# Moving weight loads, mask rows and transposes by a few chunks in a fused hash-attention and gated-MLP kernel

## The chip, the cores and the metric

The kernel runs on one core of a Trainium2 chip. The time is device microseconds (us) of one execution. It was taken five times; the median counts. One further execution was recorded by the hardware profiler, and all durations below are from that one.

## The reference, cut to what matters

Attention comes first: 4 batches of 8 heads, 768 positions, 64 numbers per head. Every query and key gets a 6-bit hash (the signs of its products with `proj`), and a query sees only the keys with its own hash. The result, regrouped as 3072 tokens of 512 numbers, goes through a gated MLP with a gated residual.

```python
q_bits = (np.einsum('bhsd,dk->bhsk', q, proj) > 0)      # the same for k
mask = q_bucket[:, :, :, None] == k_bucket[:, :, None, :]
scores = np.where(mask, scale * q @ k^T, -1e9)
attn = softmax(scores) @ v                               # then to x: 3072 x 512
...
ffn_out = (gelu(x @ w_gate) * (x @ w_val)) @ w_out
out = x + sigmoid(x @ w_res) * ffn_out
```

## The kernel before, in words

**Pairs and chunks.** Heads are taken two at a time: 16 pairs, four to a batch, numbered from 0 in the code, so the "third pair" is pair 2 and the "fifth pair" is pair 4. A pair's scores are cut into nine chunks. The main loop (L575 to L595) runs over 144 slots, one chunk each: slot 9p is the first chunk of pair p. A slot issues the score matmuls of its chunk (`scores`, L368: four or eight matmuls for the two heads into a PSUM tile `sp`, then one exponential on ScalarE into `e`), then the tasks listed for that slot, then MLP matmuls of the batch before as filling, then the product of an earlier chunk's `e` with the values (`values`, L341).

**The mask is folded into the score matmul.** Each head has 64 rows of transposed q or k and 7 more "mask rows" made of the hash bits. The first head of pair p lies in the tiles `aug[p, side]` (rows 0 to 63, mask rows from row 64), the second in `second[p % 4][side]` (rows 64 to 127, mask rows in rows 0 to 6). So a pair's first score matmuls need both `aug` tiles complete, and the next ones both `second` tiles.

**How a pair is prepared.** q and k come in by `load` (L79; DMAs of 384 KB issued from SyncE's queue, SP). GpSimd (POOL) casts them to bf16 (`cast`, L169). For pairs 4 and up a DMA transpose issued from SP puts them into `aug` (`transpose_dma`, L186), and POOL copies the second head's rows into `second` (`move_second`, L190). VectorE transposes the unrounded q and k in 32x32 blocks (`blocks`, L210), TensorE computes the hashes of two pairs at once (`hash_half`, L240), and `spread` (L265) lays the bits out in the tile `bits` with three copies on VectorE. `mask_rows` (L286 to L290) then issues four small DMAs from SP, 10.5 KB each: two into the `aug` tiles, then two into the `second` tiles. POOL's `values_prep` (L464) makes the value operand: one cast and a sum in three steps; pairs 2 and 3 sum on VectorE instead.

**What sets the order.** Nothing reorders the program: each engine and each DMA queue executes in the order written. `at(slot, f, ...)` (L448) appends a task to a slot by hand; tasks of one slot run in the order in which the `at` lines stand. An engine that waits for nothing runs ahead of the others, so the slot of a POOL or SP task gives its place in that queue and no time.

**Buffers.** `ldv` has two buffers, so the value load of pair 3 waits for POOL's sum of pair 1's values, `ld` has three, `aug` four, `second` four. SP's DMAs take eight completion semaphores in turn; an issue waits for the DMA eight places before it.

**Weights.** `load_w` (L160) issues the next of twelve MLP weight DMAs from POOL's own DMA queue: gate and value weights in four column quarters each (384 KB), the residual weights, the output weights in thirds. Four are issued early, eight in slot 39. `gate_val` (L383) first uses them in slot 39, which is the fourth slot of the second batch; the rest of the kernel alternates such gate/value stages with batches of attention that are filled up with `project` (L407).

Of the kernel before, what the change touches and what calls it, by code (L numbers as in the profile page):

```python
# [17 lines left out]
def kernel(  # L18
# [96 lines left out]
    for sides in ((0, 0, 1, 1), (0, 1, 0, 1)):  # L115
# [5 lines left out]
        for side, val in ((0, 1.0), (1, -NBITS / 4.0)):  # L121
            i, j = [j for j in range(4) if sides[j] == side]
# [325 lines left out]
    def at(slot, f, *args):  # L448
        if f in (hash_half, spread, transpose_pe):
            uses_tp.add(slot)  # L450
        tasks[slot].append(lambda: f(*args))
        busy[slot] += cost.get(f, 0.0)
# [55 lines left out]
    at(1, spread, 1, 0, 4, ROW)  # L508
    at(2, spread, 1, 4, T, TP)
    at(2, mask_rows, 1)  # L510
    at(6, values_prep, 1)

    for i in range(4):
        x = (2 + i // 2, i % 2)
# [6 lines left out]
        at(8 + dh, hash_half, 2, dh, ROW)  # L521
    for i, s in enumerate((10, 11, 12)):
        at(s, spread, 2, 4 * i, 4 * i + 4, (TP, ROW, TP)[i])
    for p in (2, 3):
        at(12, mask_rows, p)
    for p in (2, 3):
        at(6 * p - 2, values_cast, p)
        at(3 * p + 8, values_sum, p, nc.vector)
# [6 lines left out]
    for p in range(4, NPAIR, 2):  # L535
        s0 = NCH * (p - 2)
        for i in range(4):
            x = (p + i // 2, i % 2)
            at(s0 + i, cast, x)
            at(s0 + 2 + i, blocks, x)  # L540
            at(s0 + 4 + 2 * (i // 2), transpose_dma, x)
            at(s0 + 8 + i, move_second, x)
        for dh in range(2):
            at(s0 + 7 + dh, hash_half, p, dh)
        for i, s in enumerate((9, 12, 13)):
            at(s0 + s, spread, p, 4 * i, 4 * i + 4)
        at(s0 + 13, mask_rows, p)
        at(s0 + 15, mask_rows, p + 1)
        at(s0 + 12, values_prep, p)
        at(s0 + 17, values_prep, p + 1)  # L550
        at(s0 + 10, load, p + 1, (2,))
        if p + 2 < NPAIR:
            at(s0 + 5, load, p + 2, (0, 1))
            at(s0 + 8, load, p + 3, (0, 1))
            at(s0 + 15, load, p + 2, (2,))
    for s in [13, 14, 15, 16] + 8 * [39]:
        at(s, load_w)

    LEAD = 4
# [3 lines left out]
    for b in range(1, B):  # L563

        s0 = b * per_batch
# [9 lines left out]
    for s in range(NSLOT):  # L575
        p, c = divmod(s, NCH)
# [56 lines left out]
```

## Time and profile before

| what | value |
|---|---|
| median of 5 runs | 364.36 us (363.98 to 364.92) |
| the profiled execution, its time | 364.36 us |
| its span, first to last instruction | 362.6 us |
| TensorE (PE) busy | 345.4 us, 95% |
| ScalarE (ACT) busy | 211.8 us, 58% |
| VectorE (DVE) busy | 147.2 us, 41% |
| POOL busy | 123.2 us, 34% |
| mean granted TensorE clock | 0.992 |
| DMA traffic | 38.02 MB, mean 105 GB/s |

The page gives for each engine its busy time and share; below that, the span in 40 slices of 9.07 us, with a digit for the busy tenths. "PEclk" there is the clock that TensorE was granted; one slice of the first ten stands at 8 tenths, the others there at 9. In the table of groups the last column is the time in which the engine stood idle before an instruction, and what ended that. TensorE's share is 95%, so the engine itself is the limit almost everywhere, and what can be won or lost lies in the few stretches where it waits. Of the span, 1.8 us (364.36 less 362.6) lie around the first and last instruction.

### The profile page before, as it was taken

The page shows a single profiled execution, that of the slowest core. Times are in us where ns is not written, and L with a number is a line of the kernel's source. Part 1 is how long each engine was busy: PE and PEld are TensorE (multiplying, and loading weights), DVE is VectorE, ACT ScalarE, POOL GpSimd, SP SyncE. Part 2 cuts the span into 40 slices and gives each one's busy share as a digit, 9 for nine tenths or more (in the row PEclk, how much of TensorE's full clock was granted, in tenths as well). Part 3 has the DMA queues.
Part 4 walks back from the last instruction along what each step waited for, and adds up shares of the span by engine and source line. Part 5 has one row for each costly group of instructions (what it writes and reads, how often), then busy time and mean ns, then how long its engine had stood idle before and what let it go on. Part 6 is the DMA issues. An engine that isn't in the chain of part 4 may idle for free.

```text
span 362.6 us, 7415 instructions
## 1 busy us (share of the span) xinstructions
PE 345.4 (95%) x3026; PEld 203.7 (56%) x3078; DVE 147.2 (41%) x200; ACT 211.8 (58%) x234; POOL 123.2 (34%) x178
## 2 busy tenths in 40 slices
PE   8896999999999999999999999999999999999994
PEld 4554566666465566666455556665556555565442
DVE  7864544343343344333443434333442123333343
ACT  4886887324778788232877777332778875232210
POOL 7996297000448258200046457400025112000000
PEclk9999899999999999999999999999999999999998
DMA  7579929998206932920004954510002210000012
GB/s 241 197 258 184 263 102 148 185 208 176 57 23 149 266 99 79 228 107 0 2 3 126 203 168 127 119 42 2 1 2 81 63 51 31 29 2 0 31 59 85
DMA packets 50201, 38.02 MB, mean 105 GB/s; under 512 B 28244, under 2 KB 47096, under 8 KB 50168
## 3 DMA queue, kind: packets, MB, share of 16 engines
q1 hardware_dynamic: 43752, 32.31, 33.3%
q0 software_dynamic: 6336, 5.24, 9.9%
q8 instruction: 24, 0.39, 0.5%
q14 instruction: 9, 0.07, 0.1%
q10 hardware_dynamic: 80, 0.00, 0.0%
HBM read 29.36 MB, written 6.29 MB: 98 GB/s over the span
## 4 chain that ended last, share of the span: by engine, by line
PE 86%; ACT 4%; DMA 3%; DVE 2%; POOL 2%; issue 2%; SPq 0%; DVEq 0%; ACTq 0%; POOLq 0%
PE sp L393 34%; PE fps L425 17%; PE sp L374 14%; PE av L355 9%; PE rps L415 5%; PE hs L248 3%; ACT e L378 3%; DMA ld<-in_q_dram 2%; PE av L348 2%; PE spr L261 2%; DMA second<-bits 1%; POOL second L192 1%; ACT th L418 1%; PE tp L200 1%; DVE o L430 1%
## 5 line engine op out<-in xcount | busy, mean ns | idle before, releaser
L378 ACT ACTIVATE e<-sp 128x1024 bf16<-128x1024 f32 x144 | 144.8, 1024 | 39.0 <-PE sp L374 30.8
L399 ACT ACTIVATE gt<-sp 128x768 bf16<-128x768 f32 x48 | 38.9, 811 | 82.9 <-PE sp L393 82.9
L402 DVE SCALAR_TENSOR_TENSOR hh<-gt,sp 128x768 bf16<-128x768 bf16 x48 | 45.8, 954 | 81.7 <-PE sp L393 81.7
L425 PE MATMUL fps<-wo,hh 128*128 128x512 bf16 x276 | 72.8, 378 | 0.8
L393 PE MATMUL sp<-x_sb,wg 128*128 128x512 bf16 (+1 forms) x377 | 70.0, 325 | 0.5
L432 POOL TENSOR_TENSOR o<-o,x_tok 128x512 f32<-128x512 f32 x18 | 20.8, 1155 | 145.7 <-DVE o L430 81.8
L393 PE MATMUL sp<-x_sb,wv 128*128 128x512 bf16 (+1 forms) x375 | 69.8, 324 | 0.5
L355 PEld LDWEIGHTS <-e 128*128 128x128 bf16 x1152 | 52.3, 98 | 30.7 <-issue 9.4
L355 PE MATMUL av<-va,e 128*128 128x65 bf16 x1152 | 58.7, 194 | 1.0 <-ACT e L378 0.5
L374 PE MATMUL sp<-aug,aug 71*128 71x512 bf16 x192 | 55.3, 328 | 3.8 <-DMA aug<-bits 2.0
L393 PEld LDWEIGHTS <-wg 128*128 128x128 bf16 x384 | 37.4, 98 | 25.0 <-issue 0.3
L393 PEld LDWEIGHTS <-wv 128*128 128x128 bf16 x384 | 37.4, 98 | 24.5
L374 PE MATMUL sp<-second,second 128*128 128x256 bf16 (+1 forms) x172 | 47.4, 321 | 0.6 <-DMA second<-bits 0.6
L425 PEld LDWEIGHTS <-hh 128*128 128x128 bf16 x288 | 27.6, 97 | 27.6
L430 DVE SCALAR_TENSOR_TENSOR o<-th,fps 128x512 f32<-128x512 f32 x24 | 16.4, 685 | 56.2 <-PE fps L425 56.2
L192 POOL COPY second<-aug 64x768 bf16<-64x768 bf16 x32 | 25.7, 825 | 33.9 <-DMA aug<-nat 25.1
L212 DVE STREAM_TRANSPOSE t<-ld 128x768 f32<-128x768 f32 x32 | 29.5, 952 | 0.0
L415 PE MATMUL rps<-wr,x_sb 128*128 128x512 bf16 x93 | 24.4, 379 | 0.2
L418 ACT ACTIVATE th<-rps 128x512 f32<-128x512 f32 x24 | 14.3, 595 | 16.3 <-PE rps L415 13.0
L374 PEld LDWEIGHTS <-second 128*128 128x128 bf16 x192 | 18.9, 98 | 6.0 <-issue 2.4
L268 DVE CAST bits<-spr 128x512 bf16<-128x512 f32 (+1 forms) x23 | 15.4, 679 | 12.5 <-PE spr L261 12.5
L374 PEld LDWEIGHTS <-aug 71*128 71x128 bf16 x192 | 16.3, 97 | 6.6 <-DMA aug<-bits 2.1
(56 smaller groups left out, 216.6 us busy)
## 6 DMA issues: line engine op xcount, KB each, us to landing
ld<-in_q_dram SPq DMA_DIRECT2D x16, 384.0 KB
ld<-in_k_dram SPq DMA_DIRECT2D x16, 384.0 KB
ldv<-in_v_dram SPq DMA_DIRECT2D x16, 384.0 KB
out_dram<-o SPq DMA_DIRECT2D x24, 256.0 KB
wg<-in_moe_w_gate_dram POOLq DMA_DIRECT2D x4, 384.0 KB, 6.6
wv<-in_moe_w_val_dram POOLq DMA_DIRECT2D x4, 384.0 KB, 9.3
wo<-in_moe_w_out_dram POOLq DMA_DIRECT2D x3, 512.0 KB, 23.7
wr<-in_moe_w_res_dram POOLq DMA_DIRECT2D x1, 512.0 KB, 17.6
```

What stands on the lines that cost most here:

```text
L192: eng.tensor_copy(second[x[0] % NM][x[1]][D:P], aug[x][D:P])
L212: nc.vector.transpose(tt.rearrange("p c h n -> p (c h n)"), raw[x].rearrange("p c d -> p (c d)"))
L355: nc.tensor.matmul(o[:, qt, :], e[:, off:off + P], va[:, hi, jt, 0:D + 1], start=False, stop=(jt == T - 1), skip_group_check=True)
L374: nc.tensor.matmul(sp[:, off:off + nq * P], ks[0:n, jt, :], qs[0:n, qt0:qt0 + nq, :], start=True, stop=True)
L378: nc.scalar.activation(e, sp, AF.Exp, scale=float(ALPHA))
L393: nc.tensor.matmul(sp[:, c0:c1], w[:, kk, bass.ts(m, P)], xs[:, kk, c0:c1], start=(kk == 0), stop=(kk == KM - 1))
L399: nc.scalar.activation(gt, sp[:, 0:S], AF.Gelu)
L402: nc.vector.scalar_tensor_tensor(hh[:, m, :], gt, 0.5, ps[1][:, 0:S], op0=ALU.mult, op1=ALU.mult)
L415: nc.tensor.matmul(rps, x_sb[b][:, kk, t, :], wr[:, kk, :], start=(kk == 0), stop=(kk == KM - 1))
L425: nc.tensor.matmul(fps, hh[:, m, bass.ts(t, P)], wo[:, m, :], start=(m == 0), stop=(m == KF - 1))
L430: nc.vector.scalar_tensor_tensor(o, th, 1.0, fps, op0=ALU.add, op1=ALU.mult)
L432: last.tensor_add(o3, o3, x_tok[b][:, :, t, :])
```

## The change

Five places of the schedule move; no instruction is added or taken away.

```diff
-    at(6, values_prep, 1)
+    at(8, values_prep, 1)
...
-    for p in (2, 3):
-        at(12, mask_rows, p)
+    at(12, mask_rows, 2)
+    at(14, mask_rows, 3)
...
     for p in range(4, NPAIR, 2):
         s0 = NCH * (p - 2)
         for i in range(4):
             x = (p + i // 2, i % 2)
...
-            at(s0 + 4 + 2 * (i // 2), transpose_dma, x)
-            at(s0 + 8 + i, move_second, x)
+            at(s0 + (8 if p == 4 else 4) + i // 2, transpose_dma, x)
+            at(s0 + (11 if p == 4 else 8) + i, move_second, x)
...
-    for s in [13, 14, 15, 16] + 8 * [39]:
+    for s in [17, 18, 19, 20] + 8 * [39]:
         at(s, load_w)
```

What this makes of the queues, as the built program has them:

- POOL, from the second head's copy of pair 2 on. Before: copy, value cast and sum of pair 1 (four instructions), three copies, value cast of pair 2, weight loads 1 to 3, value cast of pair 3, weight load 4, four casts of pairs 4 and 5. After: three copies, value cast and sum of pair 1, one copy, value casts of pairs 2 and 3, weight load 1, cast, load 2, cast, load 3, cast, load 4, cast.
- SP: the mask rows of pairs 2 and 3 follow each other as before (no SP task lies in slots 13 and 14). Then, before: value load of pair 4, two transposes of pair 4, two loads of pair 6, two transposes of pair 5, two loads of pair 7. After: value load of pair 4, loads of pair 6, transposes of pair 4, loads of pair 7, transposes of pair 5.
- POOL's copies of pair 5 come after the value cast and sum of pair 4 instead of ahead of them.
- For pairs 6, 8, 10, 12 and 14 the transposes of the odd pair behind it (7, 9, ...) stand one slot earlier, and so ahead of the two loads of slot s0+5.

## Prediction

> **What bounds the kernel now.** I read TensorE's own waits first, then the stretches they fall in, then the time-ordered list of instructions there, then the DMA queues of that stretch. TensorE is 95% busy, so its waits are nearly all there is to win. The list of its waits over the whole run:
>
> ```profile
> PE sp L374 <- DMA aug<-bits: 2.0, 1, 2.0
> PE sp L374 <- ACT e L378: 1.5, 6, 0.4
> ...
> PE sp L374 <- DMA second<-bits: 0.6, 1, 0.6
> ```
>
> The columns are total us, times, longest. One event of 2.0 and one of 0.6 us, both for mask rows. The stretches around it (busy us of PE, PEld, DVE, ACT, POOL, then granted clock, DMA share, GB/s):
>
> ```profile
> 27.50:31.50 4.00, 3.68 (x58) 2.90 (x57) 3.27 (x3) 3.79 (x5) 3.98 (x7) 1.00 1.17 159
> 31.50:35.90 4.40, 1.75 (x23) 0.97 (x21) 0.15 (x2) 1.91 (x3) 1.53 (x2) 1.00 1.31 208
> 35.90:39.30 3.40, 3.01 (x23) 1.94 (x24) 3.37 (x5) 2.97 (x4) 0.00 (x0) 0.50 1.55 199
> ```
>
> TensorE works 1.75 of 4.40 us, and in the next 3.4 us its clock is halved. Who issued what, in order of time:
>
> ```profile
> 25.88 0.97 POOL L162 DMA_DIRECT2D wg<-in_moe_w_gate_dram  x1
> ...
> 26.68 1.53 SPq L290 DMA_DIRECT2D aug<-bits  x2
> 26.85 0.75 POOL L162 DMA_DIRECT2D wv<-in_moe_w_val_dram  x1
> ...
> 28.30 1.70 SPq L290 DMA_DIRECT2D second<-bits  x2
> ...
> 33.58 0.39 PE L374 MATMUL sp<-aug,aug 71*128 71x512 bf16 x1 [2.02 <-DMA aug<-bits]
> ...
> 34.52 0.38 PE L374 MATMUL sp<-second,second 128*128 128x512 bf16 x1 [0.55 <-DMA second<-bits]
> ```
>
> Pair 2's four mask rows are issued from 26.68 to 30.0, just after the weight loads. In the trace's completion counts they land at 31.34, 33.54, 33.75 and 34.39: 4.7 to 6.0 us after issue (26.68, 27.52, 28.30, 29.32). Pair 4's rows, issued from 49.60 in an empty stretch, land 1.9 to 2.0 us after issue. So the weights cost each row 2.7 to 4.1 us. The queues from 28 to 36 us (packets, MB, share of 16 engines):
>
> ```profile
> q0 software_dynamic: 1941, 1.45, 121.0%
> q1 hardware_dynamic: 94, 0.08, 3.7%
> ```
>
> q0 carries POOL's weights, q1 all of SP's DMAs: the rows are a trickle behind a saturated queue.
>
> **What is there to win.** TensorE was ready at 31.56 (end of the value matmuls that start at 31.16). ScalarE, the bound of this stage at 0.9 to 1.0 us per chunk, waits 2.49 us and resumes at 35.00. After that, at half clock, it waits 0.24 and 0.92 us more; some 0.3 to 0.5 of it would be there anyway (x's transposes fall there), so the clock costs about 0.8. Full prize: 2.5 + 0.8 = 3.3 us.
>
> **The change, step by step.**
>
> *When the first weight load now goes out.* POOL does not wait for slots; it runs ahead. Pair 2's first copy starts at 18.87. Now two more copies come first (0.77 each by their spacing), so pair 1's cast and sum start at 21.3 instead of 19.76, and its first sum ends at about 23.1 instead of 21.55. SP's value load of pair 3 waits for that sum: 23.1 instead of 21.58. Pair 2's load of the same kind, issued at 18.33 into idle engines, landed at 21.77, after 3.44 us; so pair 3's lands at about 26.6. POOL, free at 25.9, now waits 0.7 us for it, because the value cast of pair 3 stands ahead of the weights. The cast takes 0.77, and the first load is issued at W = 27.4 instead of 25.88. The next follow every 1.7 us (0.75 to 0.97 issue + 0.8 cast): 29.1, 30.7, 32.2. The move is four slots in the program but 1.5 us in time for the first load.
>
> *When the rows land.* SP issues pair 2's rows at the same times, since they wait for VectorE's bits (26.66). The loads of pairs 4 and 5 in q1 now end near 28.7 instead of 28.2; the first row slips behind them, to about 29. Second row, 27.52: W+0.1. The nearest row of the trace is pair 5's last mask row, issued 0.2 us after a weight load (55.12 and 54.92): it landed at 59.14, 4.0 us later, while its forerunner, issued 0.5 us ahead of the load, took 1.9. So the second row lands between 29.4 and 31.5, in time either way. The `second` rows, 28.30 and 29.1, are W+0.9 and W+1.7. With one load ahead, as pair 2's first row had it (4.7 us), they land at 33.0 and, one more turn of the queue (0.8 us by the spacing of the rows' packets), 33.4 to 33.8. Bounds for the last: 31.0 if nothing delays it, 35.1 if it gets the 6.0 us of the row that met two loads. I take 33.4: the second load is issued in the same 0.1 us, so half the contention of before.
>
> The Trainium skill speaks of a smaller delay. DMA: Bandwidth & Descriptors, section on queues, rings and completion order: each engine takes turns between queues packet by packet, about 9 to 17 descriptors each. At 79 ns per weight descriptor (the trace) a row would wait at most 1.3 us: the last row would land at 29.1 + 1.9 + 1.3 = 32.3 and the change would win 2.2 us of the stall. The rows of before waited 2.7 to 4.1; I go by them.
>
> *What TensorE does with it.* The `aug` matmul starts at 31.56, no wait. The `second` matmul starts at 33.4 instead of 34.52: 1.1 us. The idle time shrinks from 2.57 (2.02 + 0.55) to some 1.5 us, in one gap.
>
> *Does the clock still drop?* TensorE: Matmul & The Clock Gate, section on HAM oscillation, says that idle gaps must stay under about 3.4 us. By that the clock would not have dropped before either, with gaps of 2.0 and 0.55, and there would be nothing to regain here. The trace shows 0.50 for 3.4 us after them; PE was busy about half of the window before. With 1.5 us idle it is busy over that. I take it that the clock holds, at 6 in 10: +0.8 us.
>
> Sum: 1.1 + 0.8 = 1.9 us off the span, 362.6 to 360.7; with the 1.8 us around it, 362.5 us. The profiled execution's own time equals the median.
>
> *What costs nothing, and its cover.* Pair 1's value sum ends at 24.1 instead of 22.6; its first reader, TensorE, comes at 26.2: without that 2.1 us of cover each us would be a us of TensorE. Pair 3's mask rows keep their place on SP; they are read in slot 27 (about 45.9) and landed at 37.1. The weight loads of slot 39 stand after the same POOL work; wv's third quarter landed at 65.5 and is needed near 74, 6 us of cover even when TensorE comes 2 us earlier. For pairs 6 and up the odd pair's transposes move ahead of two loads; those are issued 1.2 to 13 us later (the first two at about 75 instead of 61.7) and are cast at 112. Later ones have 20 us or more (118.5 and 139.7). In those stages TensorE waits for no DMA at all.
>
> *What has less cover.* Pair 4's transposes now stand behind two loads on SP. Before, they landed near 41 and POOL's copies of pair 4 ended at 42.6. Pair 4's mask rows, which overwrite rows those copies read, are issued at 49.60, when the bits are ready; their last lands at 53.88, and TensorE reads them at 54.52: 0.6 us of cover. With TensorE 1.9 us earlier the rows fall due at 47.7. Behind the weights (ending 1.5 us later) and two loads of 1.1 us, the transposes land at about 44.5; copies end at 46.1. Cover: 1.6 us, and the 0.6 behind it.
>
> **Rivals.**
>
> *Half of it.* The last row also meets the second load, lands at 34 to 34.4, and the clock drops as before: gain 0 to 1.1 us, 363.7. For: both are issued within 0.1 us. Against: before, three loads were out by 28.3, now one. 0.25.
>
> *All of it.* Pair 3's value load lands later than I think (one of its engines came 0.8 us late before), W passes 28.5, the rows get through: 361.2. Against: the row at W'+0.2 lost 2 us even so. 0.12.
>
> *Slower: the fifth pair's rows come late.* DMA transposes issued behind loads under weight traffic were held up: 6.9 and 6.0 us at 63.0 and 70.0, against 1.3 in quiet. Behind pair 4's two transposes SP still has two loads, two transposes and a value load to issue, 4.0 us together, before pair 4's mask rows; the last of those is issued 2.4 us after the first and lands 1.9 after that. They are needed at 54.5 less 1.9 = 52.6. So the second transpose's issue may end at 52.6 - 8.3 = 44.3 without harm; past that each us is a us, and with 0.8 for the clock the gain is gone at 45.4. With both held up it ends at 34.6 + 12.9 = 47.5: 3.2 lost, plus 0.8, less 1.9: 366.5. Against: the weights end near 39.5 here, where in that stretch they lasted to 86. 0.16.
>
> *It does not do what it says*, because POOL's run-ahead undoes the move wholly (W near 26): 364.4. 0.05.
>
> **How the numbers follow.** Forecast 0.42 (361.9 to 363.1), half 0.25, all 0.12, late rows 0.16, nothing 0.05. This kernel can be told from no change at about 0.2%, 0.7 us: faster below 363.6, slower above 365.1. Faster: 0.40 + 0.11 + 0.12 = 0.63; slower 0.17; same 0.20. The range takes in "all" at its likely value and the milder half of the late rows: 361.0 to 365.2.
>
> **What would show it.** Right: the first weight issue near 27.4 behind a cast of pair 3, the `aug` matmul of slot 18 without a wait, the `second` one waiting 1 to 1.8 us, clock 1.00 up to 40 us, copies of pair 4 over by 46.5. Wrong: W before 26.5 or after 28.5; rows that land 2 us after issue although a weight load is ahead; a wait of TensorE near 52 us; or any DMA wait after 90 us.

## The result and the profile after

The changed kernel takes 363.2 us (median of 43 runs, 361.23 to 366.32). The kernel before, measured beside it, takes 364.09 us (80 runs, 363.02 to 365.7). The ratio is 0.9977, with a 95% interval from 0.9967 to 0.9986: 0.9 us faster, where 1.9 was forecast (362.5 us). The profiled execution took 363.49 us with a span of 361.7.

First TensorE's waits for the whole run:

```profile
PE sp L374 <- DMA second<-bits: 1.7, 1, 1.7
...
PE sp L374 <- ACT e L378: 1.3, 5, 0.4
```

The wait of 2.0 us for `aug<-bits` is gone. The one for `second<-bits` has grown from 0.6 to 1.7 us. Together 2.6 us became 1.7. No other wait for a DMA's mask rows has come up, at slot 36 or anywhere behind it. The same stretches as before:

```profile
27.50:31.50 4.00, 3.68 (x56) 2.83 (x56) 3.07 (x3) 3.59 (x4) 3.96 (x6) 1.00 0.93 175
31.50:35.90 4.40, 2.66 (x32) 1.59 (x29) 0.69 (x3) 2.74 (x4) 2.73 (x4) 0.87 1.20 181
35.90:39.30 3.40, 3.18 (x35) 1.99 (x35) 3.40 (x4) 2.49 (x4) 0.00 (x0) 0.67 1.22 259
```

TensorE is busy for 2.66 of the 4.40 us instead of 1.75. Yet the granted clock, the third number from the end, still falls: 0.87 and then 0.67. Who issued what, in order of time:

```profile
26.87 1.49 SPq L290 DMA_DIRECT2D aug<-bits  x2
26.95 0.83 POOL L293 CAST va<-ldv 128x768 bf16<-128x768 f32 x1 [0.81 <-DMA ldv<-in_v_dram]
...
27.72 0.97 POOL L162 DMA_DIRECT2D wg<-in_moe_w_gate_dram  x1
...
28.46 1.44 SPq L290 DMA_DIRECT2D second<-bits  x2
...
31.83 0.38 PE L374 MATMUL sp<-aug,aug 71*128 71x512 bf16 x1
...
33.87 0.39 PE L374 MATMUL sp<-second,second 128*128 128x512 bf16 x1 [1.67 <-DMA second<-bits]
...
35.43 0.58 PE L374 MATMUL sp<-aug,aug 71*128 71x256 bf16 x2
...
49.28 1.02 ACT L378 ACTIVATE e<-sp 128x1024 bf16<-128x1024 f32 x1 [0.39 <-PE sp L374]
...
57.78 1.02 ACT L378 ACTIVATE e<-sp 128x1024 bf16<-128x1024 f32 x1 [0.54 <-PE sp L374]
```

The first weight load goes out at 27.72, behind the cast that waits 0.81 us for pair 3's values. In the completion counts the `aug` rows land at 29.74 and 29.94, in time; the `second` rows at 33.65 and 33.83, which is 5.2 and 4.6 us after their issue. The two matmuls at 35.43 take 0.58 us together instead of 0.38, as the same pair does at 30.91: that is the reduced clock.

**A ruler for all the runs.** The last two of these lines are the exponentials of slots 31 and 39. In the kernel before they stand at

```profile
50.16 1.02 ACT L378 ACTIVATE e<-sp 128x1024 bf16<-128x1024 f32 x1 [0.39 <-PE sp L374]
...
58.66 1.02 ACT L378 ACTIVATE e<-sp 128x1024 bf16<-128x1024 f32 x1 [0.54 <-PE sp L374]
```

Profiles differ by up to 1.2 us in when pair 2's mask rows are ready (first issue from 25.81 to 26.99). So I count from that issue: 23.48 and 31.98 us before, 22.41 and 30.91 after. By slot 31 the change has gained 1.07 us, and by slot 39 it still has 1.07. The span shows 0.9, since the rows were issued 0.19 later in this profile. The slot of a reader shows what was won at slot 18; the later one shows what was given back at slot 36, where pair 4's mask rows are first read.

| kernel | gained by slot 31, us | by slot 39, us | median us (runs) | ratio to before [95%] |
|---|---|---|---|---|
| the change | 1.07 | 1.07 | 363.2 (43) | 0.9977 [0.9967, 0.9986] |
| e1_loads_only | 2.35 | -1.55 | 363.87 (14) | 0.9991 [0.9969, 1.0013] |
| e2_no_transposes | 0.96 | 0.95 | 363.49 (14) | 0.9991 [0.9974, 1.0008] |
| e3_fifth_pair_only | -0.38 | -0.38 | 363.88 (14) | 0.9995 [0.9983, 1.0007] |
| e4_loads_behind_copies | 3.70 | 0.84 | 365.14 (22) | 1.0035 [1.0015, 1.0054] |
| e5_loads_plus_late_kv | 1.24 | 1.24 | 362.97 (22) | 0.9961 [0.9947, 0.9976] |
| e6_gate_late_kv | 3.70 | 0.80 | 364.22 (22) | 1.0004 [0.9991, 1.0017] |
| e7_after_filler | 2.47 | 1.79 | 362.58 (22) | 0.9964 [0.9947, 0.998] |
| e8_after_late_kv | 1.11 | 1.11 | 362.85 (22) | 0.9972 [0.9953, 0.9991] |
| e9_loads_kv_filler | 2.11 | 2.10 | 361.5 (5) | 0.9933 [0.9921, 0.9945] |
| e10_before_filler | 0.83 | 0.82 | 363.01 (13) | 0.9969 [0.9959, 0.9978] |
| e11_after_kv_filler | 2.07 | 2.06 | 362.77 (12) | 0.9961 [0.9943, 0.9979] |
| e12_late_loads_late_kv | 3.70 | 2.36 | 361.9 (7) | 0.9943 [0.9916, 0.997] |

The gains are of one profiled execution each, the medians and ratios of many. Each kernel was timed beside runs of the kernel before, whose medians lay between 364.09 and 364.36. Two of the 22 runs of e4 (368.5 and 368.93) lay over 1.5% above its fastest and stand in its median, but not in its ratio.

### The profile page after: what moved, and what is told of

The parts are those of the page before. It is cut to its first block, busy times and chain, and to the rows that moved or that the text cites. A ratio compares the mean times of both kernels' runs of the same rounds, so it can differ in the third digit from the quotient of the medians.

```text
span 361.7 us, 7415 instructions
## 1 busy us (share of the span) xinstructions
PE 345.3 (95%) x3026; PEld 203.4 (56%) x3078; DVE 147.2 (41%) x200; ACT 211.8 (59%) x234; POOL 123.5 (34%) x178
## 4 chain that ended last, share of the span: by engine, by line
PE 87%; ACT 4%; DMA 3%; DVE 2%; POOL 2%; issue 2%; SPq 0%; DVEq 0%; ACTq 0%; POOLq 0%
PE sp L393 34%; PE fps L425 17%; PE sp L374 14%; PE av L355 9%; PE rps L415 5%; PE hs L248 3%; ACT e L378 3%; DMA ld<-in_q_dram 2%; PE av L348 2%; PE spr L261 2%; DMA second<-bits 1%; POOL second L192 1%; ACT th L418 1%; PE tp L200 1%; DVE o L430 1%
## 5 line engine op out<-in xcount | busy, mean ns | idle before, releaser
L355 PEld LDWEIGHTS <-e 128*128 128x128 bf16 x1152 | 52.3, 98 | 30.7 <-issue 9.4
```

Of the source, the lines that this page charges most:

```text
L355: nc.tensor.matmul(o[:, qt, :], e[:, off:off + P], va[:, hi, jt, 0:D + 1], start=False, stop=(jt == T - 1), skip_group_check=True)
```

## The experiments

My theory after the result: the stall at slot 18 is the mask rows' wait behind the weights. What the change should have won beyond 1.07 us went to the halved clock, which the remaining idle time still triggers. Rivals: part of the gain is given back at slot 36 by the fifth pair's late rows; or the part that moves the transposes takes it away.

### Which part does it?

**e1_loads_only**, the weight loads alone:

```diff
-    for s in [13, 14, 15, 16] + 8 * [39]:
+    for s in [17, 18, 19, 20] + 8 * [39]:
```

> Only the first four weight loads move (slots 17 to 20); value sum of pair 1, mask rows and transposes stay as before. Theory A (the rows of pair 2 land earlier because fewer weight loads are queued ahead of them): pair 3's value load keeps its issue at 21.6 us and lands near 26.1, so the first weight load goes out near 26.9 instead of 27.7 with the whole change; it meets all four rows of pair 2, and TensorE's `second` matmul of slot 18 starts between 33.9 and 34.5. Gain 0 to 0.6 us, less than the whole change. Theory B (the gain comes from the order of transposes and loads on SP): no gain, 0.0 us, `second` matmul at 34.5. If the loads' slots alone carry the change: the same 0.9 us.

Slot 18 gains more than in the whole change, and more than I had expected, 2.35 us: the `second` wait is 1.3 us, and the clock held in this execution. Then slot 36 takes it all away. SP's queue and TensorE there:

```profile
45.01 0.53 SPq L88 DMA_DIRECT2D ld<-in_q_dram  x1
45.64 0.42 SPq L88 DMA_DIRECT2D ld<-in_k_dram  x1
46.11 0.46 SPq L88 DMA_DIRECT2D ldv<-in_v_dram  x1
46.67 1.56 SPq L290 DMA_DIRECT2D aug<-bits  x2
...
53.09 0.61 PE L374 MATMUL sp<-aug,aug 71*128 71x512 bf16 x1 [2.02 <-DMA aug<-bits]
```

```profile
50.00:60.00 10.00, 7.68 (x70) 4.99 (x68) 3.52 (x5) 5.58 (x7) 9.62 (x14) 0.66 0.48 141
```

Pair 4's rows are issued right behind three loads of pairs 7 and 5. The loads land at 50.46, 51.48 and 52.64, the rows only at 52.83 to 53.44. From 46 to 54 no weights were under way. So the rows stand in line behind loads of their own queue. Those loads were late themselves, since pair 5's transposes held SP from 40.58 to 44.92. The wait is 2.02 us, and the mean clock of this 10 us stretch is 0.66.

**e2_no_transposes**, everything but the transposes and copies of pair 4 and up:

```diff
-    at(6, values_prep, 1)
+    at(8, values_prep, 1)
...
-    for p in (2, 3):
-        at(12, mask_rows, p)
+    at(12, mask_rows, 2)
+    at(14, mask_rows, 3)
...
-    for s in [13, 14, 15, 16] + 8 * [39]:
+    for s in [17, 18, 19, 20] + 8 * [39]:
```

> The whole change without its transposes and copies: loads, pair 1's value sum and pair 3's rows move, the transposes of pair 5 and of all later pairs stay as before. Theory A: all of the gain is here, about 0.9 us (ratio 0.9975), with the first weight load near 27.7 us and the `second` matmul of slot 18 near 33.9. Theory B: no gain. If the transposes cost something by delaying the second group of weight loads, this one is faster than the whole change by some tenths.

**e3_fifth_pair_only**, the transposes and copies of pairs 4 and 5 alone:

```diff
-            at(s0 + 4 + 2 * (i // 2), transpose_dma, x)
-            at(s0 + 8 + i, move_second, x)
+            at(s0 + (8 + i // 2 if p == 4 else 4 + 2 * (i // 2)), transpose_dma, x)
+            at(s0 + (11 if p == 4 else 8) + i, move_second, x)
```

> Only pair 4's and 5's transposes and copies move four (and three) slots back; the weight loads stay as before. Theory A: the rows of pair 2 land as before, `second` matmul at 34.5 us, time within 0.3 us of before, or slower if the copies of pair 4 end after 48 us and its mask rows come late (TensorE then waits near 54 us). Theory B: a gain of 0.5 us or more.

e2 has 0.95 of the 1.07 us in its profile, the same single wait (1.9 us for `second<-bits`), and none at slot 36. e3 keeps the wait for `aug<-bits` (2.2 us) and gains nothing. The gain sits in the loads. The value sum's move adds little: in e1, without it, the first weight load goes out 0.77 us after the first row's issue, in the change 0.85. These are readings of the profiles; in the runs alone, the interval of e2 reaches past 1. What the transposes add is too little to measure here: the intervals of e2 and of the change overlap. The earlier transposes of pairs 7, 9 and so on were not tested by themselves.

### What is there to win if the rows meet no weights?

**e4_loads_behind_copies**, the kernel before with the four loads behind pair 4's copies:

```diff
-    for s in [13, 14, 15, 16] + 8 * [39]:
+    for s in 4 * [27] + 8 * [39]:
```

> Before, with the first four weight loads in slot 27, behind POOL's copies of pair 4, which can only start when its transposes have landed; so no weight load is out before about 37 us. Theory A: pair 2's rows land 1.9 us after issue, at 28.6 to 31.2, TensorE does not wait for them at all, the clock stays at 1.00 to 45 us, and the whole prize of 3.3 us is taken: about 361 us, ratio 0.991, unless the loads now make pair 4's rows late (TensorE waiting near 51 us, then 1 to 2 us less). Theory B: no gain from this.

```profile
27.05 8.46 ACT L378 ACTIVATE e<-sp 128x1024 bf16<-128x1024 f32 x9 [0.80 <-PE sp L374]
...
51.38 0.39 PE L374 MATMUL sp<-aug,aug 71*128 71x512 bf16 x1 [1.51 <-DMA aug<-bits]
...
52.58 0.59 PE L374 MATMUL sp<-second,second 128*128 128x512 bf16 x1 [0.81 <-DMA second<-bits]
```

ScalarE now runs nine exponentials in one go through slot 18. With no weight load out, the rows land 1.9 us after issue (27.95 for the one issued at 26.02). That settles the cause of the stall. It was worth 3.70 us, more than the 3.3 I had worked out. Slot 36 takes 2.9 of it back here: with the first weight load at 38.17, the rows of pair 4 meet both the weights and the loads of their own queue. Over its runs this kernel is 0.35% slower. Its profiled execution was the quickest of them, so where the slower ones lost time is not seen. The nine above 366 us have a mean clock of 0.985 to 0.991, the profiled one 0.993, so part of it was clock.

### Does the second deadline decide?

**e5_loads_plus_late_kv** is e1 with the three loads behind pair 4's rows:

```diff
-            at(s0 + 17, values_prep, p + 1)
-            at(s0 + 10, load, p + 1, (2,))
+            at(s0 + (24 if p == 4 else 17), values_prep, p + 1)
+            at(s0 + (15 if p == 4 else 10), load, p + 1, (2,))
...
-            at(s0 + 8, load, p + 3, (0, 1))
+            at(s0 + (16 if p == 4 else 8), load, p + 3, (0, 1))
```

> The run with the weight loads alone, and besides that pair 7's q and k loads and pair 5's value load (with its sum on POOL) stand behind the mask rows of pairs 4 and 5 on SP. Theory A (what is won at slot 18 is given back at slot 36, where pair 4's rows queue behind these three loads): pair 4's rows land 1.9 to 2.5 us after issue, TensorE does not wait near 53 us, and the 1 to 2.3 us won at slot 18 stay: 362 to 363 us, 1 to 2 us less than with the loads alone. Rival (pair 4's rows are late because of POOL's copies or the weights, not because of these loads): the wait near 53 us stays, time as with the loads alone, 363.9 us.

The only wait for rows that is left in the list:

```profile
PE sp L374 <- DMA second<-bits: 1.2, 1, 1.2
```

Slot 36 is free; nothing of the 1.24 us is given back. Pair 4's rows, issued from 48.33 on, land 1.9 to 2.0 us after their issue, although pair 5's transposes held SP for 4.52 us here too. In e1 the first took 6.2 us. The ratio is 0.9961 against e1's 0.9991; the intervals overlap a little (0.9969 to 0.9976), so it is these landings and the wait that is gone that decide: in e1 the loads ahead in the queue were the cause. Slot 18 won less here than in e1 although the wait is the same (1.2 and 1.3 us): here the clock fell to 0.67 in the stretch from 35.9 to 39.3.

**e8_after_late_kv** puts the same three lines into the changed kernel.

> The whole change, with pair 7's loads and pair 5's value load behind the rows of pairs 4 and 5. Theory A: in most executions the change only just meets the deadline at slot 36 and in some it misses it (its slow tail, up to 366.3 us); without the three loads ahead the tail goes, the median falls by 0.3 to 0.8 us to about 362.6. Rival: no difference, 363.2 us with the same tail.

It gains 1.11 us in both slots, and its ratio can't be told from that of the change. The changed kernel's own rows were in time, so there was nothing to free. The executions above 365 us, which I had put down to this deadline, are still there.

**e6_gate_late_kv** is the kernel before with those three lines and, ahead of the weights, a small POOL copy. It reads the value sum of pair 3, which VectorE ends at 30.92 here, and so holds the weights back until pair 2's rows are through:

```diff
+    gate = const.tile([P, 1], BF16, name="gate")
+    at(18, nc.gpsimd.tensor_copy, gate, vals[3][1][:, 0, 0:1])
-    for s in [13, 14, 15, 16] + 8 * [39]:
+    for s in 4 * [18] + 8 * [39]:
```

> As the run before, but the first four weight loads stand behind a one-column copy on POOL that reads the value sum of pair 3, which VectorE ends near 31.6 us. Theory A: no weight load before 31.6, pair 2's rows land by 31.2, no wait at slot 18, clock 1.00 there; pair 4's rows no longer queue behind the three loads; the whole prize of 3 to 3.5 us: about 361 us, ratio 0.991, and a narrower spread than the whole change (361.2 to 366.3). Rival: a wait near 51 us takes 1.5 us or more back, 362.5 us or slower.

My main forecast was wrong by 3 us, and the rival held. Slot 18 is free and 3.70 us are gained, but:

```profile
39.52 8.37 SPq L187 DMA_TRANSPOSE aug<-nat  x2
48.07 1.56 SPq L290 DMA_DIRECT2D aug<-bits  x2
```

The weights, first issued at 31.11, now run under pair 5's transposes. These hold SP's queue for 8.37 us, against 2.57 in e4, where no weight data moved yet. Whether the weights alone make that difference is not shown: in the kernel before, pair 4's transposes held SP for only 2.79 us (33.67 to 36.46) with weights under way. Pair 4's rows leave at 48.07, and TensorE waits 1.6 and 0.6 us for them at slot 36.

**e12_late_loads_late_kv** is e5 with e4's place for the loads (`4 * [27] + 8 * [39]`).

> The weight loads behind pair 4's copies as in e4 (no wait at slot 18, clock kept there, 3.7 us gained by slot 31), and the three loads of pairs 5 and 7 moved behind pair 4's mask rows as in e5. In e4 those rows were issued at 45.2 and landed at 50.8 to 52.4, due at 49.9; both the three loads in their own queue and the weights in POOL's queue (38.2 to 55) were under way. If the loads in their own queue delayed them, they now land some 2 to 3.5 us after issue, before 49.9: no wait at slot 36, and the time is 364.2 less up to 3.7: 360.5 to 361.5. If the weights delayed them, as they did pair 2's rows before the change, they land 4.7 to 6 us after issue again, the wait of 1.5 us at slot 36 stays, and the time is 363 to 365, as in e4.

```profile
45.83 1.56 SPq L290 DMA_DIRECT2D aug<-bits  x2
47.44 1.43 SPq L290 DMA_DIRECT2D second<-bits  x2
...
51.38 0.39 PE L374 MATMUL sp<-aug,aug 71*128 71x512 bf16 x1 [0.93 <-DMA aug<-bits]
...
52.34 0.38 PE L374 MATMUL sp<-second,second 128*128 128x512 bf16 x1 [0.57 <-DMA second<-bits]
```

Behind the weights alone the first row lands at 50.63, 4.8 us after its issue, as pair 2's did. So the weights delay these rows too. The loads in their own queue cost the rest: the wait is 1.5 us instead of e4's 2.3. The clock stays at 1.00 from 50 to 60 us instead of 0.83. That is in part luck: the two gaps lie on either side of 51.65, a point where the clock could change (see the part on the prediction). Neither side of my expectation held alone: the wait stayed, and the time fell to 361.9.

### Is the halved clock a cost of its own?

Seven useless matmuls in slot 17, whose product nobody reads, fill the gap without moving a row:

```diff
+    at(17, warm_up, 7, ROW)
```

**e7_after_filler**, the changed kernel with this line:

> The whole change plus seven matmuls without use (0.22 us each, 1.5 us) at the end of slot 17, where TensorE waits for pair 2's rows anyway; they add work that is not in the reference and change no result. If the clock drop costs what the prediction said: the clock stays at 1.00 through 40 us and the run is 0.5 to 0.8 us faster than the whole change, 362.5 us. If the half clock costs nothing, because ScalarE is the bound there, or if it comes from elsewhere: the same 363.2 us, or up to 0.4 slower. If a gain at slot 18 is only given back at slot 36: a new wait near 52 us and the same 363.2 us.

```profile
31.50:35.90 4.40, 3.83 (x41) 2.18 (x40) 1.48 (x4) 3.28 (x5) 2.81 (x4) 1.00 1.25 177
35.90:39.30 3.40, 3.40 (x56) 2.59 (x55) 3.40 (x5) 3.24 (x4) 0.00 (x0) 1.00 1.21 255
```

The clock holds, and 2.47 us are won by slot 31. At slot 36 the rows, issued at 47.19 and landing at 52.3 to 52.9, are now 0.7 us late.

**e10_before_filler**, the kernel before with this line and nothing else:

> The kernel before, with the seven useless matmuls in slot 17 and nothing else. They shorten no wait for the mask rows (rows land near 33.5 and 34.4 as before); they only keep TensorE busy while it waits. If the half clock is a cost of its own, set by how idle TensorE is in the window, the clock rises from 0.50 to near 1.00 in the stretch from 35.9 to 39.3 and the time falls by 0.4 to 0.8: about 363.5. If seven (some 2 us at their 0.3 each) don't fill a gap of 2.6 us, or the half clock costs nothing because ScalarE is the bound there, it stays at 364.1.

```profile
30.40 1.67 PE L167 MATMUL wps<-warm,eps_sb 128*128 128x512 bf16 x7
32.81 0.39 PE L374 MATMUL sp<-aug,aug 71*128 71x512 bf16 x1 [0.49 <-DMA aug<-bits]
...
34.04 0.38 PE L374 MATMUL sp<-second,second 128*128 128x512 bf16 x1 [0.84 <-DMA second<-bits]
```

```profile
35.90:39.30 3.40, 3.03 (x45) 2.22 (x45) 3.40 (x5) 3.23 (x4) 0.00 (x0) 1.00 1.50 204
```

This is the clean measurement. The rows come no earlier: ScalarE resumes 8.59 us after the first row's issue, 8.32 in the kernel before. The clock goes from 0.50 to 1.00 in this stretch. 0.83 us are gained by slot 31 although the stall is 0.27 us longer, so the clock was worth 1.1 us; the ratio of 0.9969 is 1.1 us too. Seven matmuls without use win as much as the whole change (0.9977; the intervals overlap).

**e9_loads_kv_filler** (e5 with this line) and **e11_after_kv_filler** (e8 with it):

> The weight loads' move, pair 4's rows freed of the loads ahead of them (as in e5), and seven matmuls without use in slot 17. If the half clock and the queue behind the fifth pair's rows are two separate costs, both are gone: TensorE waits 1.2 us at slot 18 less the 0.4 to 0.6 that the useless matmuls fill, no wait at slot 36, clock 1.00 throughout; the time is the 362.97 of e5 less about 0.6: 362.3 to 362.5, and the times above 364 become rare. If the two are one cost, since what is won in slot 18 is given back in slot 36 whatever is done, the time stays at 362.9 or above and a wait for aug<-bits stands at slot 36.

> The whole change, pair 4's rows freed as in e8, and the useless matmuls as in e7. In e7 a wait of 0.7 us appeared at slot 36 once the clock held. If the loads in SP's queue cause it, it goes here, and the time is the 362.6 of e7 less 0.3 to 0.7: 362.1. If pair 4's late transposes cause it (they hold SP), the wait stays and the time is that of e7, 362.6, and above that of e9.

In both, one wait for rows remains. That of e9 in its list of waits:

```profile
PE sp L374 <- DMA second<-bits: 0.2, 1, 0.2
```

The clock is 1.00 up to 60 us, and the 2.1 us won by slot 31 are all there at slot 39. e9 takes 361.5 us (five runs), 0.67% less than before and better than I expected. It beats the kernel before and the changed one. e11 gains the same in its profile but takes 362.77 us in the median; some of its executions at full clock took over 363, and what they waited for is open. The wait of e7 at slot 36 is gone in e11's profile, which speaks for the loads in SP's queue as its cause. Its time, though, is what I had forecast for the rival, pair 4's late transposes, and the profiled execution was one of its quickest. So the runs leave that rival open.

## Why the prediction was right in sign and half in size

**When the first weight load goes out: right.** 27.4 was forecast, 27.72 came, behind the cast as worked out; of the difference, 0.19 is the later start of this stage.

**When the rows land, and what TensorE does with it: right within what executions differ by.** The `aug` matmul doesn't wait, and one gap of 1.67 us is left where 1.0 to 1.8 was said. ScalarE resumes 7.49 us after the first row's issue, 8.32 before: 0.83 us where the sum had 1.1. Four more executions with loads and value sum in this place (e2, e7, e8, e11) resume after 7.70, 6.95, 7.35 and 7.35, a gain of 0.6 to 1.4. The Trainium skill's rule (DMA: Bandwidth & Descriptors, on queues, rings and completion order), from which I had estimated a delay of at most 1.3 us, would have had the rows at 32.3. They came at 33.83; the rows of the trace before were the better guide. My "at most" was wrong: 17 descriptors is the page's typical packet, and it allows up to 64, by the same estimate 5.1 us, so these landings do not contradict it.

**Does the clock still drop: wrong.** This is the step that failed, "I take it that the clock holds, at 6 in 10: +0.8 us". It dropped in the profiled execution: what came back was 1.07 less 0.83, or 0.24 us. A stretch of 3.4 us at half clock takes 1.7 us off 362, so one such stretch shows as a mean clock of 0.995. Only 11 of 44 executions of the changed kernel have 0.997 or more (the profiled one has 0.995); their median is 362.05, near the forecast. The 24 at 0.993 to 0.996 have 363.32, and the 9 below 364.58. Of 163 executions of the kernel before that were measured beside the experiments, none is above 0.995. So the chance was nearer 1 in 4 than 6 in 10. This is a rough count: the mean does not say where a drop lay, and one at the very end, where TensorE has no work left, lowers it too. The size was 1.1 rather than 0.8 us (e10): of ScalarE's waits of 0.24 and 0.92 us, 0.17 remain at full clock, and I had left 0.3 to 0.5.

My reason, "With 1.5 us idle it is busy over that" (half), was met in the stretch that I had looked at (2.66 of 4.40 us) and not in the one that counts. In the traces' clock records the changes lie on a grid: full and half stretches last 3.41 us or a multiple of it (half: 3.41 or 6.83; full: 27.3 to 355), up to the end of the span. Cut along that grid, the stretches with the gap and those behind them read, for the kernel before, the change, e1 and e5:

```profile
32.51:35.92 3.41, 1.69 (x20) 0.97 (x21) 0.06 (x1) 0.92 (x2) 0.52 (x1) 1.00 1.32 210
35.92:39.34 3.42, 3.05 (x24) 1.98 (x25) 3.38 (x5) 2.95 (x4) 0.00 (x0) 0.50 1.53 196
...
31.33:34.74 3.41, 1.67 (x22) 0.87 (x21) 0.48 (x1) 1.75 (x3) 2.90 (x4) 1.00 1.18 175
34.74:38.16 3.42, 3.20 (x23) 1.97 (x23) 2.65 (x4) 3.18 (x4) 0.00 (x0) 0.50 1.26 239
...
31.82:35.23 3.41, 2.21 (x24) 1.45 (x26) 1.41 (x3) 2.30 (x3) 1.35 (x2) 1.00 1.19 167
...
31.32:34.74 3.42, 1.89 (x28) 1.00 (x25) 0.49 (x2) 2.24 (x4) 2.62 (x4) 1.00 1.22 164
```

The change has less idle time in all, but its one gap (32.20 to 33.87) lies wholly in one stretch, and TensorE is busy there no longer than before: 1.67 us against 1.69. So the clock drops again. In e1 the gap (31.19 to 32.46) lies across the border at 31.82, TensorE is busy for 2.21 us, and the clock stays at 1.00 behind it. In e5 a gap of nearly the same length lies within one stretch, and the clock falls to 0.50 at 34.74. From 26 to 60 us of the 14 profiles, a stretch at full clock was followed by half clock when TensorE was busy for 1.27 to 1.89 of its 3.41 us (nine cases), and not once when it was busy for 2.07 us or more. Where the grid lies differs from one profile to the next (compare the borders above). So whether a gap of this length costs the clock is in part luck, and 6 in 10 was a guess on the wrong stretch.

The limit of 3.4 us for a gap in the Trainium skill (TensorE: Matmul & The Clock Gate, HAM oscillation) doesn't cover it: here single gaps of 1.20 us (e5) and 1.67 us (the change) were enough.

**The rivals.** "Half of it" had the right clock and nearly the right time: 363.7 against 363.2. "Late rows": the mechanism is real, and showed at full size in e6, e1 and e4, but the change stays short of it. Pair 4's two transposes took 6.79 us, close to the 6.9 feared, but pair 5's only 3.08, and the rows, issued at 48.73, landed at 52.2 to 52.9, in time. That was so in part because the clock had dropped: in e7, where it held, they were 0.7 us late. I had priced only the time in which transposes hold SP. e1 and e5 showed a second way: the loads ahead of the rows in SP's queue still have their data to move when the rows are issued. "All of it" had 3.3 us as the full prize; e4 shows 3.7 by slot 31.

**What was costed at nothing** cost nothing that can be seen: no wait of TensorE for a DMA comes up behind slot 36, and e2, which leaves the transposes of all pairs in place, can't be told from the change.

What stays open: whether busy time is what the clock follows. The line between 1.89 and 2.07 us holds from 26 to 60 us only. At the end of the span, where other matmuls run, five profiles kept the clock behind a stretch with 1.4 to 2.0 us busy (the change: 1.49 from 355.59 on).

## What to carry to other kernels

A stall on TensorE can cost twice: the gap, and a stretch at half clock behind it. Look at how busy TensorE is between the points where the clock can change, and price the second cost by an experiment that fills the gap with useless matmuls, and do that early; here it won as much as the reordering. When a stall is shortened, ask which later deadline had slack only because of the stall: here a small DMA behind large loads in one queue (e1), or behind another queue's weights (e12), came late as soon as its reader came early. A gain of 3.7 us at one place was worth nothing until the next place was freed, and the two best versions, e9 and e12 (0.9933 and 0.9943, which their intervals don't tell apart), each treat the rows of slot 18 and the queue ahead of slot 36 together.

## What the runs showed of the hardware

- Half clock for 3.41 us behind gaps of only 1.20 and 1.67 us (e5, the change), when the gap lay in one stretch of the clock's grid; none behind 1.27 us across two stretches (e1).
- A mask row of 10.5 KB lands 1.9 us after issue in quiet (e4, slot 18), 4.6 to 5.2 us behind another queue's weights (the `second` rows of the change; 4.8 for the first row of e12), and up to 6.2 us behind three loads of its own queue (e1: issued at 46.67, the first landed at 52.83).
- Two DMA transposes held SP's queue for 2.57 us in quiet (e4), but for 2.79 (before, pair 4's) and 8.37 us (e6) with weights under way, and the next DMA on SP was issued only after them. What makes the difference between the last two is open.
